# Attention into a two-layer MLP: tile 5's second layer by seven block products within tile 6's first layer, batches 4 to 7 prepared ahead, casts of v by ScalarE

## The chip, the cores and the metric

The kernel runs on one core of one Trainium2 chip. The metric is the device time of one execution in microseconds; the time of a kernel is the median of its runs. A profile is one more execution, taken by the hardware profiler; its times are in microseconds from the start of its span.

## The reference

Eight batches of eight heads, 576 positions of 64 channels, all inputs fp32. The softmax of q runs over the channels and that of k over the positions, so attention is two small products per head; the result, 4608 tokens of 512 features, goes through two dense layers with a leaky ReLU between them.

```python
q_s = np.exp(q - np.max(q, axis=-1, keepdims=True))
q_s = q_s / (np.sum(q_s, axis=-1, keepdims=True) + 1e-09)
k_s = np.exp(k - np.max(k, axis=2, keepdims=True))
k_s = k_s / (np.sum(k_s, axis=2, keepdims=True) + 1e-09)
kv = np.einsum('bhsd,bhse->bhde', k_s, v)
attn_out = np.einsum('bhsd,bhde->bhse', q_s, kv)
x = attn_out.transpose(0, 2, 1, 3).reshape(B * S, H * D)   # 4608 x 512
h = x @ w_in                                               # w_in 512 x 2048
g = np.maximum(0.01 * h, h)
out = g @ w_out                                            # w_out 2048 x 512
```

## The kernel before

**The dense layers.** The 4608 tokens are nine tiles of 512 (TT). x is kept transposed in SBUF as `xT`, bf16. Layer 1 of a tile is 16 block rows j of four matmuls each (128x512, bf16, L563); after each block row ScalarE applies the leaky ReLU into a tile of `g_pool` (L572). Layer 2 is four blocks of 128 tokens (tsub) with 16 matmuls of 128x512 each (L584, driven by `layer2_at`, L983); after the sixteenth, ScalarE copies the bank to `out_sb` (L578) and SyncE issues two stores of 128 KB (L581). Tile 0 has an order of its own, tiles 1 to 5 run layer 1 and then layer 2 this way, and tile 6 only its layer 1. Tiles 7 and 8 are computed as a pair with Strassen-like products of 2x2 blocks (products at L998, tail at L1252). Such a scheme takes seven block products where the plain one takes eight; its sums of blocks need an fp32r operand. Tile 6's second layer is computed by seven block products too, in 112 matmuls of 256 columns (`fill_steps`, L1156 to L1165): two of the products are plain, in bf16, and five use a sum of blocks of g (6r1 to 6r4, 6c22) with a sum of blocks of `w_out` (v1 to v4, and o22, a copy). They fill gaps of the first layer of the pair.

**The attention of a batch.** Its steps are functions that each issue instructions to one engine:

- `load_all` (SyncE): k, q and v of a batch into the six buffers of `raw_pool`.
- `k_begin`, `k_tree` (VectorE, L160): the maximum of k, first by a tree of elementwise maxima over four halvings.
- `k_allmax` (VectorE, L167 to L190): the maximum across partitions, by transposes within blocks; then `k_sub` (VectorE, L198) and `k_exp` (ScalarE, L206), which leaves `ke`.
- `q_max` (L245), `q_sub` (L304) on VectorE, `q_exp` on ScalarE (L312), `q_sum` (L321) and `q_norm` (L328) on VectorE, which leave `qe`; `q_turn` then transposes `qe` into `qX` by a DMA transpose on SyncE's queue (L551).
- `v_cast`: v to bf16 in two halves, on GpSimd (L218) for most batches.
- `attend_kv(b)` (TensorE): k·v of batch b+1 (L341), and between its parts q·kv of batch b (L479). Then `kd_make` on VectorE (L361, L362) divides k·v by its sums, and ScalarE casts the result of batch b to `xT` (`x_keep`, L500). One PSUM tile, `pokv`, holds part of both, and `x_keep` reads it after `kd_make` has.

Inside `attend_kv(b)`, `ke` of b+1 is asked for at once and `qX` of b after the first 24 matmuls.

**The order.** Everything around the dense layers is placed by hand. `at(t, u, ...)` (L595) hangs functions on a slot, and `run(t, u)` (L600) issues them there. Slots u = 0 to 15 of tile t lie after block row u of layer 1; slots 16 + 4·tsub + j//4 lie in layer 2 after each fourth matmul, so a tile has 32. The instructions of each engine run in the order of issue, and an engine that waits holds back all that stands behind it; the loads, the transposes and the stores of the output share SyncE's one queue. The slots of each batch are set on L699 to L784: for batches 4 and 5 a loop over t = 3, 4 with the helpers `k_front` (L740), `q_front`, `casts` and `q_back`, for 6 and 7 by single lines. For the last three batches `attend_kv` stands at slot 23 of tiles 3, 4 and 5, and batch 7's attention at (5, 29).

**What the end of the kernel prepares.** The weight sums (`out_weight_tiles` L807, `out_weight_sums` L812, `in_weight_sums`, the last on GpSimd), the token sums of the pair (`token_sums`, L844) and the sums of tile 6's g (`six_sums`, `six_first`) hang on slots of tiles 5 and 6. `home` (L863) takes an fp32r buffer for a sum, and `spent(n)` (L793) names parts of `xT` whose tokens are no longer read, which take blocks of g near the end.

Of the kernel before, what the change touches and what calls it, by code (L numbers as in the profile page):

```python
# [20 lines left out]
L = 64  # L21
# [5 lines left out]
def kernel(  # L27
# [31 lines left out]
    g_pool = ctx.enter_context(tc.tile_pool(name="gsb", bufs=10))  # L59
# [752 lines left out]
    def out_weight_sums(*names):  # L812
        w = lambda fh, os: w_out_sb[:, fh * NH : (fh + 1) * NH, os]
        for n in names:
            if n == "o22":
                nc.gpsimd.tensor_copy(out=late["o22"], in_=w(1, E2))
                continue
            x, y = dict(
                v1=lambda: (w(0, E2), w(0, E1)),
                v2=lambda: (w(1, E2), plain("v1")),  # L820
                v3=lambda: (w(1, E2), w(0, E2)),
                v4=lambda: (w(1, E1), plain("v2")),
            )[n]()
            subtract(nc.vector, n, x, y)
# [19 lines left out]
    def token_sums():  # L844
# [4 lines left out]
        for n in ("s1", "s2", "s3", "s4", "a22"):  # L849
            late[n] = pool.tile([P, 2, TT], F32R, name=n)  # L850
        nc.vector.tensor_tensor(out=late["s1"], in0=xT[:, CL, XB], in1=xT[:, CR, XB], op=ALU.add)
# [14 lines left out]
    def six_blocks(h):  # L866
        hs = slice(h * M2, (h + 1) * M2)
        return [(slice(2 * k, 2 * k + 2), lambda fh, k=k: late["g6"][4 * fh + k][:, :, hs]) for k in range(4)]

    def six_sums(n, k):  # L870
        (ms, h0), (_, h1) = six_blocks(0)[k], six_blocks(1)[k]
        part = lambda n: late[n][:, ms].bitcast(FP32)
        if n == "c22":
            nc.scalar.copy(out=late["6c22"][:, ms], in_=h1(1))
            return
        x, y, op = dict(
            r1=lambda: (h1(0), h1(1), ALU.add),
            r2=lambda: (part("6r1"), h0(0), ALU.subtract),
            r3=lambda: (h0(0), h1(0), ALU.subtract),
            r4=lambda: (h0(1), part("6r2"), ALU.subtract),  # L880
        )[n]()
        eng = nc.vector if n in ("r1", "r2") else nc.gpsimd
        eng.tensor_tensor(out=late["6r2" if n == "r4" else "6" + n][:, ms], in0=x, in1=y, op=op)

    def six_first(k):
        if k == 0:
            home("6r1", "alpha")
            home("6r2", "beta")
        six_sums("r1", k)
        six_sums("r2", k)  # L890

    for n in range(3):
        at(6, 10 + 2 * n, lambda n=n: six_first(n))
    at(6, 14, lambda: pair_first(0))

    def g_tiles():
        return [g_pool.tile([P, 2, TT], BF16, name="gj") for _ in range(NF // 2)]
# [114 lines left out]

    for t in range(1, TA):
        g_sb = []
        for j in range(NF):
            ph = psB_pool.tile([P, TT], FP32, name="ph", tag=BANK_TAG)
            layer1(j, ph, t * TT, TT)
            if j % 2 == 0:
                g_sb.append(g_pool.tile([P, 2, TT], BF16, name="gj"))
                if t == TA - 1:  # L1020
                    late["g6"] = g_sb
            leaky(g_sb[j // 2][:, j % 2], ph)
# [10 lines left out]
    def g7_rows(i):  # L1033
        if i == 0:
            g7_pairs.extend(g_pool.tile([P, 2, TT], BF16, name="gj") for _ in range(2))
        for fh in range(2):
            if i < 2:
                g7[fh * NH + i] = g7_pairs[fh][:, i]
            elif i < 6:
                g7[fh * NH + i] = spent(4 * (4 + fh) + i - 2)  # L1040
# [3 lines left out]
    def g7_blocks(h):  # L1044
# [3 lines left out]
            (slice(2, 4), lambda fh: xT[:, 0:2, ts(4 + fh)]),  # L1048
            (slice(4, 6), lambda fh: xT[:, 2:4, ts(4 + fh)]),
            (slice(6, 8), lambda fh: xT[:, 2 * fh : 2 * fh + 2, ts(6)]),  # L1050
        )

    def g7_wide(h):
        b = g7_blocks(h)
        ts = lambda t: slice(t * TT + h * M2, t * TT + (h + 1) * M2)
        return b[0], (slice(2, 6), lambda fh: xT[:, :, ts(4 + fh)]), b[3]
# [11 lines left out]
    def sums_ahead(n, names=("r1",)):  # L1068
        if n == 0 and "r1" in names:
            home("r1", "beta")  # L1070
            late["r3lo"] = late["ahead"].tile([P, NH // 2, M2], F32R, name="r3lo")
        if n == 2 and "r3" in names:
            home("r3", "alpha")
# [13 lines left out]
    def pair_layer1(i, fills):  # L1087
# [17 lines left out]
        else:  # L1105
            six_first(3)
# [21 lines left out]
        if i + 2 < NH:  # L1128
            in_weight_sums(i + 2)
        if i == 1:  # L1130
            home("6r3", "alpha")
        for n in {1: (0, 1), 2: (2, 3)}.get(i, ()):
            six_sums("r3", n)
        for n in {3: range(4)}.get(i, ()):
            six_sums("r4", n)
# [13 lines left out]
    early, late_in = {}, {}  # L1149

    def put(o, t, half, i, cols, issues=(nc.sync, nc.sync)):
        for n, issue in enumerate(issues):
            b, c = divmod(t * TT + half * M2 + i * P + n * L, S)
            issue.dma_start(out=out_r[b, c // L, :, cols], in_=o[n * L : (n + 1) * L, cols])

    def fill_steps():  # L1156
        t, g = TA - 1, lambda n: late["g6"][n // 2][:, n % 2]
        o1, o2 = ([osb_pool.tile([P, O], FP32, name="out_sb") for _ in range(2)] for _ in range(2))
        bank2 = lambda: psO_pool.tile([P, 2, H2], FP32, name="pout", tag="pout")
        pw, py = bank2(), bank2()  # L1160

        def steps(ps, a, w, first=True):
            for i in range(2):
                for m in range(NH):
                    nc.tensor.matmul(  # L1165
                        ps[:, i],
                        lhsT=a(m)[:, i * P : (i + 1) * P],
                        rhs=w(m),
                        start=(first and m == 0 and i == 0),
                        stop=(m == NH - 1 and i == 1),  # L1170
                        skip_group_check=True,
                    )
                    if (i, m) != (1, NH - 1):
                        yield

        rows = lambda n: (lambda m: late[n][:, m])
        w_first = lambda fh: (lambda m: w_out_sb[:, fh * NH + m, E1])
        yield from steps(pw, lambda m: g(NH + m)[:, 0:M2], w_first(1))
        for i in range(2):
            nc.scalar.copy(out=o1[i][:, E1], in_=pw[:, i])  # L1180
        yield
        yield from steps(py, rows("6r1"), rows("v1"))
        yield
        px = bank2()
        yield from steps(px, lambda m: g(m)[:, 0:M2], w_first(0))

        def six_c11():
            for i in range(2):
                add(o1[i][:, E1], px[:, i], o1[i][:, E1])

        early[3] = six_c11
        yield
        yield from steps(px, rows("6r2"), rows("v2"), False)
        for i in range(2):
            nc.scalar.copy(out=o1[i][:, E2], in_=px[:, i])
        yield
        yield from steps(px, rows("6r3"), rows("v3"), False)
        for i in range(2):
            nc.scalar.copy(out=o2[i][:, E2], in_=px[:, i])

        def six_c22():
            for i in range(2):
                add(o2[i][:, E2], py[:, i], o2[i][:, E2])

        def six_cast():
            home("6c22", "alpha")
            for n in range(4):
                six_sums("c22", n)

        early[5], late_in[5] = six_c22, six_cast  # L1210
        yield
        yield from steps(py, rows("6r2"), rows("o22"), False)

        def six_c12():
            for i in range(2):
                add(o1[i][:, E2], py[:, i], o1[i][:, E2])
                put(o1[i], t, 0, i, slice(0, O))

        late_in[7] = six_c12
        yield  # L1220
        yield from steps(px, rows("6c22"), rows("v4"), False)
        for i in range(2):
            nc.scalar.copy(out=o2[i][:, E1], in_=px[:, i])
            put(o2[i], t, 1, i, slice(0, O))
        yield

    fill = fill_steps()
# [33 lines left out]
    def row_sums(wide, name, n, pool, op, x, y, eng=nc.vector):  # L1261
        if n == "r3":
            home("r3", "alpha")
# [13 lines left out]
    gu = lambda: g_pool.tile([P, 2, H2], FP32, name="gu", tag="gj")  # L1277
# [139 lines left out]
```

## Time and profile before

| | |
|---|---|
| time, median of 3 runs | 277.43 us (277.17 to 277.5) |
| the profiled execution's own time | 277.72 us |
| its span | 275.8 us |
| tile 3: layer 1, layer 2 | 105.89 to 119.70, to 134.81 |
| tile 4: layer 1, layer 2 | 134.81 to 148.62, to 163.73 |
| tile 5: layer 1, layer 2 | 163.73 to 177.54, to 193.37 |
| tile 6: layer 1 begins | 193.37 |

The times of the tiles are where the pieces of the chain of waits begin, in the profiled execution. How to read the rows that follow in the prediction: a row of the chain gives a start, a length, the engine, the output's name, the line, and how many instructions it joins; a row of an engine's timeline gives start, length, engine, line, operation and the names with their shapes, and in brackets the idle time before it and what ended that. In a row that groups instructions the three numbers are the shortest, the median and the longest duration in ns. "DMA to landing" is the time from the issue of a transfer to its completion.

### The profile page before, as it was taken

The page shows a single profiled execution, that of the slowest core. Times are in us where ns is not written, and L with a number is a line of the kernel's source. Part 1 is how long each engine was busy: PE and PEld are TensorE (multiplying, and loading weights), DVE is VectorE, ACT ScalarE, POOL GpSimd, SP SyncE. Part 2 cuts the span into 40 slices and gives each one's busy share as a digit, 9 for nine tenths or more (in the row PEclk, how much of TensorE's full clock was granted, in tenths as well). Part 3 has the DMA queues.
Part 4 walks back from the last instruction along what each step waited for, and adds up shares of the span by engine and source line. Part 5 has one row for each costly group of instructions (what it writes and reads, how often), then busy time and mean ns, then how long its engine had stood idle before and what let it go on. Part 6 is the DMA issues. An engine that isn't in the chain of part 4 may idle for free.

```text
span 275.8 us, 5326 instructions
## 1 busy us (share of the span) xinstructions
PE 268.4 (97%) x2041; PEld 156.3 (57%) x2066; DVE 220.8 (80%) x314; ACT 175.8 (64%) x322; POOL 89.9 (33%) x102
## 2 busy tenths in 40 slices
PE   8899999999999999999999999999999999999994
PEld 3478644444444544445444544454446777889994
DVE  2995995899999939984979799966997756669961
ACT  3977573785389366846486656854766767984241
POOL 2866470149103001200600069400001999840000
PEclk9999999999999999999999999999999999999999
DMA  6999999987998599069707956027100000025244
GB/s 236 337 209 320 242 273 244 390 275 242 235 382 292 50 347 346 16 133 391 231 0 141 384 190 126 0 49 153 39 0 0 2 0 2 1 52 117 62 107 124
DMA packets 40568, 46.48 MB, mean 168 GB/s; under 512 B 18912, under 2 KB 24288, under 8 KB 40544
## 3 DMA queue, kind: packets, MB, share of 16 engines
q1 hardware_dynamic: 36720, 41.56, 50.5%
q0 software_dynamic: 3504, 4.20, 8.7%
q10 hardware_dynamic: 320, 0.39, 0.4%
q8 instruction: 16, 0.26, 0.4%
q14 instruction: 8, 0.07, 0.1%
HBM read 36.70 MB, written 9.44 MB: 167 GB/s over the span
## 4 chain that ended last, share of the span: by engine, by line
PE 93%; DVE 3%; DMA 2%; issue 1%; ACT 0%; SPq 0%
PE ph L563 35%; PE pout L584 30%; PE pq L1252 9%; PE pp L998 9%; PE pout L1165 5%; DMA k_raw<-in_k_dram 2%; PE po L479 2%; DVE t L160 1%; PE pokv L341 1%; PE pkv L341 1%; PE pkv L419 0%; DVE k_raw L410 0%; ACT ke L206 0%; DVE kmax L160 0%; DVE kd L434 0%
## 5 line engine op out<-in xcount | busy, mean ns | idle before, releaser
L563 PE MATMUL ph<-xT,w_in_sb 128*128 128x512 bf16 (+1 forms) x504 | 98.4, 352 | 0.4
L584 PE MATMUL pout<-w_out_sb,gj 128*128 128x512 bf16 x371 | 84.6, 379 | 0.9 <-issue 0.3
L563 PEld LDWEIGHTS <-w_in_sb 128*128 128x128 bf16 x512 | 49.8, 98 | 47.0 <-DMA w_in_sb<-in_moe_w_in_dram 0.3
L572 ACT ACTIVATE gj<-ph 128x512 bf16<-128x512 f32 x112 | 63.6, 601 | 19.2 <-PE ph L563 18.6
L584 PEld LDWEIGHTS <-gj 128*128 128x128 bf16 x384 | 36.7, 98 | 43.6 <-issue 0.2
L218 POOL CAST vb<-v_raw 128x1152 bf16<-128x1152 f32 x13 | 19.2, 1505 | 81.7 <-DMA v_raw<-in_v_dram 64.5
L578 ACT COPY out_sb<-pout 128x512 f32<-128x512 f32 x20 | 11.7, 584 | 30.3 <-PE pout L584 19.1
L206 ACT ACTIVATE ke<-k_raw 128x2304 bf16<-128x2304 f32 (+2 forms) x13 | 18.0, 1385 | 7.2 <-DVE k_raw L198 6.7
L328 DVE TENSOR_TENSOR qe<-qe,qrec 128x2304 bf16<-128x2304 bf16 (+5 forms) x13 | 21.8, 1680 | 0.4
L321 DVE TENSOR_REDUCE qsum<-qe 128x36 f32<-128x2304 bf16 (+5 forms) x13 | 20.0, 1541 | 2.4 <-ACT qe L312 2.2
L245 DVE TENSOR_REDUCE qmax<-q_raw 128x36 f32<-128x2304 f32 (+5 forms) x13 | 20.0, 1539 | 0.8 <-DMA q_raw<-in_q_dram 0.8
L312 ACT ACTIVATE qe<-q_raw 128x2304 bf16<-128x2304 f32 (+5 forms) x13 | 17.2, 1321 | 4.3 <-POOL q_raw L304 3.4
L198 DVE TENSOR_TENSOR k_raw<-k_raw,kall 128x1152 f32<-128x1152 f32 (+2 forms) x10 | 18.7, 1885 | 0.3
L304 POOL TENSOR_TENSOR q_raw<-q_raw,qmax 128x512 f32<-128x512 f32 (+3 forms) x7 | 11.8, 1682 | 21.2 <-DVE qmax L245 19.3
L799 POOL TENSOR_TENSOR t<-w_in_sb 128x256 fp32r<-128x256 bf16 x16 | 15.5, 971 | 0.0
L500 ACT CAST xT<-po 128x448 bf16<-128x448 f32 (+3 forms) x31 | 13.3, 513 | 2.5 <-PE po L479 2.5
L1095 DVE COPY u<-pp 128x512 f32<-128x512 f32 x8 | 5.5, 691 | 10.9 <-PE pp L998 10.9
L998 PE MATMUL pp<-s,t 128*128 128x512 f32 x48 | 13.9, 398 | 0.0
L160 DVE TENSOR_TENSOR t<-t 128x256 f32<-128x256 f32 (+2 forms) x22 | 13.3, 605 | 0.7
L304 DVE TENSOR_TENSOR q_raw<-q_raw,qmax 128x2304 f32<-128x2304 f32 (+1 forms) x6 | 13.2, 2202 | 0.2
L1124 POOL COPY gate<-u 128x1 f32<-128x1 f32 x1 | 0.2, 189 | 37.5 <-DVE u L1001 37.5
L160 DVE TENSOR_TENSOR t<-k_raw 128x512 f32<-128x512 f32 (+1 forms) x11 | 11.2, 1015 | 1.3 <-DMA k_raw<-in_k_dram 1.2
(155 smaller groups left out, 381.3 us busy)
## 6 DMA issues: line engine op xcount, KB each, us to landing
out_dram<-out_sb SPq DMA_DIRECT2D x60, 128.0 KB, 3.9
k_raw<-in_k_dram SPq DMA_DIRECT2D x8, 576.0 KB, 6.0
v_raw<-in_v_dram SPq DMA_DIRECT2D x8, 576.0 KB, 8.9
q_raw<-in_q_dram SPq DMA_DIRECT2D x4, 1152.0 KB, 9.1
v_raw<-in_v_dram SPq DMA_DIRECT2D x4, 1152.0 KB, 11.8
k_raw<-in_k_dram SPq DMA_DIRECT2D x4, 1152.0 KB, 6.7
q_raw<-in_q_dram SPq DMA_DIRECT2D x4, 576.0 KB, 7.7
w_in_sb<-in_moe_w_in_dram POOLq DMA_DIRECT2D x7, 256.0 KB, 6.8
```

The costliest lines, as they stand in the source:

```text
L160: nc.vector.tensor_tensor(out=o, in0=i0, in1=i1, op=ALU.max)
L198: eng.tensor_tensor(out=ks, in0=ks, in1=st[b]["kall"][:, hs].unsqueeze(2).to_broadcast([P, n, R, D]), op=ALU.subtract,)
L218: eng.tensor_copy(out=o, in_=i)
L245: nc.vector.tensor_reduce(out=o, in_=st[b]["q"][:, hs, rs], axis=AX.X, op=ALU.max)
L304: eng.tensor_tensor(out=qs, in0=qs, in1=st[b]["qmax", rs.start, hs.start].unsqueeze(3).to_broadcast([P, m, n, D]), op=ALU.subtract,)
L321: nc.vector.reduce_sum(out=qsum, in_=q_cols(b, rs, hs), axis=AX.X)
L328: nc.vector.tensor_tensor(out=qes if out is None else out, in0=qes, in1=st[b]["qrec", rs.start, hs.start].unsqueeze(3).to_broadcast([P, n, ...
L563: nc.tensor.matmul(ph, lhsT=w_in_sb[:, cb, j * P : (j + 1) * P], rhs=xT[:, cb, c0 : c0 + n], start=(cb == 0 and first), stop=(cb == NB - 1 ...
L572: nc.scalar.activation(out=o, in_=ph, func=AF.Prelu, alpha=LEAKY_SLOPE)
L584: nc.tensor.matmul(pout, lhsT=g_sb[j // 2][:, j % 2, tsub * P : (tsub + 1) * P], rhs=w_out_sb[:, j, os], start=(j == 0), stop=(j == NF - 1),)
L998: nc.tensor.matmul(ps, lhsT=w(c), rhs=a(c), start=(first and c == 0), stop=(c == 1), skip_group_check=True)
L1252: nc.tensor.matmul(ps[i], lhsT=a(m)[:, i * P : (i + 1) * P], rhs=w(m), start=(first and m == 0 and (each or i == 0)), stop=(m == NH - 1 an ...
```

## The change

Tile 5's second layer is no longer 64 matmuls of 128x512 in four blocks. It is the seven products that tile 6 has, now by one function for both (`seven_steps`): 112 matmuls of 256 columns, 32 plain in bf16 and 80 with fp32r sums. Eight of them follow tile 5's layer 1, then batch 7's attention, then 24 more; the other 80 come in groups of 16 behind block rows 5, 7, 9, 12 and 14 of tile 6's layer 1. The sums of tile 5's g (5r1 to 5r4) are made by VectorE and 5c22 by ScalarE. Tile 5's g is kept in the parts of `xT` that tiles 0 to 3 have left (`spent`), the second half of tile 6's g in those of tiles 4 and 5; `g_pool` becomes three pools of 4, 4 and 2 buffers, which also take some of the sums. Some of tile 6's sums move from VectorE to GpSimd.

The slots of batches 4 to 7 move. `attend_kv(4)`, `(5)` and `(6)` go from slot 23 of tiles 3, 4 and 5 to (3, 18), (4, 17) and (4, 28); the maximum of k is taken one to several slots earlier, and `k_max(7)` at (4, 9) stands ahead of `q_ready(6)`. Load 6 goes to (3, 8) and load 7 to (3, 31), both in the order k, v, q; `q_turn(4)` and `q_turn(5)` stand directly ahead of them, `q_turn(6)` at (4, 20) behind tile 4's first store, `q_turn(7)` at (5, 9). The casts of v of batches 5, 6 and 7 and the copy o22 go from GpSimd to ScalarE.

```diff
-    g_pool = ctx.enter_context(tc.tile_pool(name="gsb", bufs=10))
+    g_pools = [ctx.enter_context(tc.tile_pool(name=f"gsb{n}", bufs=b)) for n, b in enumerate((4, 4, 2))]
...
-    for t in range(3, B - 3):
-        b = t + 1
-        q_front(b, t - 1, 29)
-        at(t, 2, lambda b=b: q_exp(b, ALLR))
-        k_front(b + 1, t, 1, 8)
-        casts(b + 1, t, 6)
-        at(t, 17, lambda b=b: k_exp(b + 1, ALLH))
-        at(t, 23, lambda b=b: attend_kv(b))
-        q_back(b, t, 5)
-        at(t, 5, lambda b=b: load_all(b + 2))
-    q_front(6, 4, 18)
-    at(4, 26, lambda: q_exp(6, ALLR))
-    k_front(7, 4, 29, 40)
-    q_back(6, 5, 1)
-    q_front(7, 5, 2)
-    casts(7, 5, 6)
-    at(5, 12, lambda: q_exp(7, ALLR))
-    q_back(7, 5, 16)
-    at(5, 17, lambda: k_exp(7, ALLH))
-    at(5, 23, lambda: attend_kv(6))
+    def k_max(b, t, u):
+        at(t, u, lambda: k_begin(b), lambda: q_begin(b), lambda: k_tree(b, ALLH))
+
+    def k_less(b, t, u):
+        at(t, u, lambda: k_allmax(b), lambda: k_sub(nc.vector, b, ALLH))
+
+    def q_ready(b, t, u):
+        at(t, u, lambda: q_sum(b, ALLR), lambda: q_norm(b, ALLR))
+
+    def casts_act(b, *slots):
+        for gg, (t, u) in enumerate(slots):
+            at(t, u, lambda gg=gg: v_cast(nc.scalar, b, gg))
+
+    q_front(4, 2, 20)
+    k_max(5, 2, 28)
+    at(2, 30, lambda: q_exp(4, ALLR))
+    q_ready(4, 2, 30)
+    casts_act(5, (3, 4), (3, 8))
+    at(3, 8, lambda: q_turn(4), lambda: load_all(6, "kvq"))
+    k_less(5, 3, 8)
+    at(3, 14, lambda: k_exp(5, ALLH))
+    q_front(5, 3, 14)
+    at(3, 18, lambda: attend_kv(4))
+    k_max(6, 3, 19)
+    at(3, 20, lambda: q_exp(5, ALLR))
+    q_ready(5, 3, 20)
+    casts_act(6, (3, 28), (3, 30))
+    at(3, 31, lambda: q_turn(5), lambda: load_all(7, "kvq"))
+    k_less(6, 3, 31)
+    at(4, 4, lambda: k_exp(6, ALLH))
+    q_front(6, 4, 4)
+    at(4, 9, lambda: q_exp(6, ALLR))
+    k_max(7, 4, 9)
+    q_ready(6, 4, 9)
+    at(4, 17, lambda: attend_kv(5))
+    k_less(7, 4, 18)
+    at(4, 20, lambda: q_turn(6))
+    casts_act(7, (4, 20), (4, 22))
+    at(4, 24, lambda: k_exp(7, ALLH))
+    q_front(7, 4, 24)
+    at(4, 28, lambda: attend_kv(6))
+    at(5, 0, lambda: q_exp(7, ALLR))
+    at(5, 0, lambda: out_weight_tiles(), lambda: out_weight_sums("v1"))
+    q_ready(7, 5, 0)
+    at(5, 9, lambda: q_turn(7))
...
-                nc.gpsimd.tensor_copy(out=late["o22"], in_=w(1, E2))
+                nc.scalar.copy(out=late["o22"], in_=w(1, E2))
...
-    at(5, 26, out_weight_tiles, lambda: in_weight_sums(0), lambda: in_weight_sums(1))
-    at(5, 26, lambda: out_weight_sums("o22", "v1"))
+    at(5, 10, lambda: out_weight_sums("v2", "v3"))
+    at(5, 12, lambda: in_weight_sums(0), lambda: in_weight_sums(1))
+    at(6, 3, lambda: out_weight_sums("o22"))
...
-    at(5, 29, lambda: attend_all(B - 1, (R7, both), (RE, both)), token_sums)
-    at(6, 4, lambda: out_weight_sums("v2", "v3", "v4"))
...
+    at(6, 0, lambda: five_sums("5r3"), lambda: out_weight_sums("v4"))
+    at(6, 5, lambda: five_steps(16))
+    at(6, 6, lambda: five_sums("5r4", "alpha"), token_sums)
+    at(6, 7, lambda: five_steps(16))
+    at(6, 8, lambda: five_sums("5c22", "beta"))
+    at(6, 9, lambda: five_steps(16))
+    at(6, 10, lambda: spare("6r1"), lambda: seven_sums("6r1", 0))
+    at(6, 12, lambda: five_steps(16), lambda: seven_sums("6r1", 1), lambda: six_second(0))
+    at(6, 14, lambda: five_steps(16), lambda: seven_sums("6r1", 2), lambda: six_second(1))
     at(6, 14, lambda: pair_first(0))
...
+        pw = bank2()
+        yield from steps(pw, lambda m: g(NH + m)[:, 0:M2], w_first(1))
+        keep_all(o1, E1, pw)
+        yield
+        if late_first:
+            px = bank2()
+            yield from steps(px, lambda m: g(m)[:, 0:M2], w_first(0))
+            add_all(o1, E1, px)
+            yield
+        py = bank2()
+        yield from steps(py, rows("r1"), v("v1"))
...
+        yield from steps(px, rows("r2"), v("v2"), False)
+        keep_all(o1, E2, px)
+        yield
+        yield from steps(px, rows("r3"), v("v3"), False)
...
+        yield from steps(py, rows("r4"), v("o22"), False)
...
+        yield from steps(px, rows("c22"), v("v4"), False)
...
     for t in range(1, TA):
...
             layer1(j, ph, t * TT, TT)
...
+            if t == TA - 2:
+                leaky(spent(j), ph)
+            elif t == TA - 1 and j >= NH:
+                leaky(spent(16 + j - NH), ph)
...
             run(t, j)
-        for tsub in range(NTS if t < TA - 1 else 0):
+        for tsub in range(NTS if t < TA - 2 else 0):
             for _ in layer2_at(t, g_sb, tsub):
                 pass
+        if t == TA - 2:
+            five = seven_steps(t, spent, late_first=True)
+            five_steps = lambda n: [next(five) for _ in range(n)]
+            five_steps(8)
+            attend_all(B - 1, (R7, both), (RE, both))
+            late_pools()
+            five_sums("5r1", "alpha")
+            five_sums("5r2", "beta")
+            five_steps(24)
...
+        if i == 0:
+            six_second(2, nc.gpsimd)
+            six_second(3, nc.gpsimd)
         if i == 1:
...
+            home("6r3", "beta")
+            for n in range(4):
+                seven_sums("6r3", n, nc.gpsimd)
+        if i == 3:
+            late["6r4"] = late["6r2"]
+            for n in range(4):
+                seven_sums("6r4", n, nc.gpsimd)
```

More of the change, by code (lines that the diff above doesn't have):

```diff
@@ L863, in home, with spare @@
     def home(n, buf):
         late[n] = late["ahead"].tile([P, NH, M2], F32R, name=n, tag=buf)
-    def six_blocks(h):
-        hs = slice(h * M2, (h + 1) * M2)
[L868 to L874, printed above, removed]
+    def spare(n):
+        late[n] = [g_pools[1].tile([P, 2, M2], F32R, name=n, tag="gj") for _ in range(NH // 2)]
@@ L1034, in g7_rows @@
         if i == 0:
-            g7_pairs.extend(g_pool.tile([P, 2, TT], BF16, name="gj") for _ in range(2))
+            g7_pairs.extend(gj(8) for _ in range(2))
+        if i == 2:
+            late["g7"] = [gj(4) for _ in range(4)]
         for fh in range(2):
@@ L1039, in g7_rows @@
             elif i < 6:
-                g7[fh * NH + i] = spent(4 * (4 + fh) + i - 2)
+                g7[fh * NH + i] = late["g7"][2 * fh + (i - 2) // 2][:, i % 2]
             else:
@@ L1105, in pair_layer1 @@
         else:
-            six_first(3)
+            seven_sums("6r1", 3)
         between(fills[0])
@@ L1147, in pair_third @@
         add(u2, py, u2)
[L1149 to L1225, printed above, removed]
@@ L1227 @@
-    fill = fill_steps()
+    fill = seven_steps(TA - 1, g6)
     def between(n):
@@ L1262, in row_sums @@
         if n == "r3":
-            home("r3", "alpha")
+            home("r3", "beta")
         else:
```

167 lines of the change are left out of this document (129 added, 38 removed).

## The prediction

> **What bounds the kernel now.** I read the page's busy shares first, then the chain that ended last, then that chain over tiles 3 to 7 in order of time.
>
> ```profile
> span 275.8 us, 5326 instructions
> PE 268.4 (97%) x2041; PEld 156.3 (57%) x2066; DVE 220.8 (80%) x314; ACT 175.8 (64%) x322; POOL 89.9 (33%) x102
> PEclk9999999999999999999999999999999999999999
> PE 93%; DVE 3%; DMA 2%; issue 1%; ACT 0%; SPq 0%
> 119.70 4.53 PE pout L584 x21
> ...
> 134.81 4.10 PE ph L563 x19
> ...
> 148.62 1.08 PE pout L584 x5
> ...
> 155.53 0.31 PE pokv L341 x24
> ...
> 157.04 0.05 issue
> ...
> 163.73 4.10 PE ph L563 x19
> ...
> 177.54 1.08 PE pout L584 x5
> ...
> 190.92 0.61 PE po L479 x16
> ...
> 193.37 0.65 PE ph L563 x3
> ```
>
> TensorE is the bound: 97% busy at the full granted clock, and 93% of the chain. In the stretch that the change touches, the chain holds nothing but PE work and pieces of "issue" of 0.05 us; no transfer and no other engine is late there. So time is won only by shorter PE work, and lost as soon as one operand arrives after PE asks for it. Three lengths come from these rows. Layer 1 of tile 4 is 64 matmuls in 148.62 - 134.81 = 13.81 us, 0.216 each. Its layer 2 takes 163.73 - 148.62 = 15.11, of which 64 x 0.216 = 13.82 are matmuls; the other 1.29 is one attend_kv. Tile 5's second layer, 177.54 to 193.37, is again 13.82 plus an attend_kv and batch 7's attention.
>
> **PE work: the gain.** Tile 5's 64 second-layer matmuls become 112 of 256 columns, 32 in bf16 and 80 with an fp32r weight and token operand (r1·v1, r2·v2, r3·v3, r4·o22, c22·v4). Tile 6 already runs both kinds:
>
> ```profile
> 219.95 1.76 PE pout L1165 x16
> ...
> 224.90 1.92 PE pout L1165 x16
> ...
> 230.03 1.92 PE pout L1165 x16
> ```
>
> The first row is a bf16 group, 1.76/16 = 0.110 each; the others are fp32r, 1.92/16 = 0.120. New cost 32 x 0.110 + 80 x 0.120 = 13.12; removed 13.82: **-0.7 us**. Nothing else is taken from PE: both attend_kv and the attention of batch 7 only move.
>
> By the Trainium skill, "TensorE: Matmul & The Clock Gate", section "Back-to-back issue gap", a matmul's gap depends on its columns alone, N/2.4 + 2.5 ns, 109 ns at 256; the fp32r rows above disagree by 11 ns each, and the measurement decides. By that rule the 112 would take 12.2 and the gain would be 1.6 us, an estimate from the page, and the forecast below would come out 0.9 lower.
>
> **What hides the new side work.** ACT takes six casts of v (each half of k_exp's elements, so about 1.1 us by its 2.12 below) and the o22 copy; it is 64% busy and the casts stand in second layers, where it has few rows to evict. DVE takes 5r1 to 5r4, 8 x 1024 elements at 1.22 (the row at 84.30), and four adds of 256, about 12 us in all, within the 13.1 us of the products and the 13.8 of tile 6's layer 1 between which they lie. PE reaches the product of r4 behind 80 of the 112 and 13 of tile 6's block rows, some 21 us after tile 5's layer 1; by the same 1.22 steps, with the sums of w_out and of tokens that stand between, r4 is done about 1 us before. I cost them at nothing. If VectorE's sums were stretched as the tree at 108.27 was beside POOL's casts (below, 4.42 in place of 2.78), 5r4 would be about 1 us late; but those casts leave POOL, which speaks against it, and POOL has little else to do there.
>
> **Preparing ahead: where a wait comes in.** Batches 4 to 7 move up by up to a tile, and each keeps a queue in front of it. I laid SP, DVE and ACT out in the new order from tile 3 on, with these durations:
>
> ```profile
> 84.30 1.22 DVE L160 TENSOR_TENSOR t<-k_raw 128x1024 f32<-128x1024 f32 x1
> ...
> 87.08 2.54 DVE L321 TENSOR_REDUCE qsum<-qe 128x36 f32<-128x2304 bf16 x1
> ...
> 90.08 2.56 DVE L328 TENSOR_TENSOR qe<-qe,qrec 128x2304 bf16<-128x2304 bf16 x1
> 92.55 0.44 DVE L167 STREAM_TRANSPOSE kmaxT<-kmax 128x256 f32<-128x256 f32 x1
> ...
> 102.40 0.17 DVE L361 RECIPROCAL krec<-pokv 128x2 f32<-128x2 f32 x1 [4.06 <-PE pokv L479]
> ...
> 103.21 2.54 DVE L245 TENSOR_REDUCE qmax<-q_raw 128x36 f32<-128x2304 f32 x1
> ...
> 108.27 1.22 DVE L160 TENSOR_TENSOR t<-k_raw 128x1024 f32<-128x1024 f32 x1
> ...
> 112.69 2.54 DVE L321 TENSOR_REDUCE qsum<-qe 128x36 f32<-128x2304 bf16 x1
> ...
> 118.16 0.43 DVE L167 STREAM_TRANSPOSE kmaxT<-kmax 128x256 f32<-128x256 f32 x1
> ...
> 120.46 2.56 DVE L198 TENSOR_TENSOR k_raw<-k_raw,kall 128x2304 f32<-128x2304 f32 x1
> ```
>
> Starts give steps: tree 2.78 (84.30 to 87.08), q_sum with its reciprocal 3.00, q_norm 2.47, kd 0.81 (102.40 to 103.21), lanes of k 2.30 (118.16 to 120.46), k_sub 2.56.
>
> The first late thing is **k of batch 7**. Load 7 is issued on SP at (3,31), the last hook of tile 3, behind tile 3's last stores and behind q_turn(5):
>
> ```profile
> 125.67 10.94 SPq L581 DMA_DIRECT2D out_dram<-out_sb  x8
> 145.78 2.71 SPq L551 DMA_TRANSPOSE qX<-qe  x1
> 148.53 1.10 SPq L84 DMA_DIRECT2D k_raw<-in_k_dram  x2
> ```
> ```profile
> L84 SPq DMA_DIRECT2D k_raw<-in_k_dram x2: 467/524/582, 148.5 to 149.2; - x2
> ...
> DMA to landing us min/median/max: 4.8/5.3/5.7
> ```
>
> The stores end at 136.61. In the trace a transpose at 145.78 has the second half of k behind it on the ground at 149.2 + 5.7 = 154.9, 9.1 later; so k7 is there at 136.6 + 9.1 = 145.7. In the hand-written order its tree stands on DVE at (4,9) ahead of q_sum(6). DVE is free for it at about 143.3 (attend_kv(4) starts behind 12 second-layer matmuls, 119.70 + 2.6 = 122.3, and its kd(4) ends 1.29 + 0.81 later at 124.4; then tree(6), q_sum(5), q_norm(5), lanes, k_sub, q_max, q_sub by the steps above, some 19 us), so it waits about 2.4 us. Behind it queue q_sum(6), q_norm(6), kd(5), k_sub(7), and behind kd(5) on ACT the copies out of the shared PSUM tile and tile 4's first output, and behind that on SP q_turn(6).
>
> 145.7 + tree 2.78 + q_sum 3.00 + q_norm 2.47 = 154.0; kd(5) ends 154.8; lanes 157.1; k_sub(7) 159.7; k_exp(7) on ACT:
>
> ```profile
> 123.05 2.12 ACT L206 ACTIVATE ke<-k_raw 128x2304 bf16<-128x2304 f32 x1 [2.71 <-DVE k_raw L198]
> ...
> 157.79 0.70 ACT L500 CAST xT<-pokv 128x256 bf16<-128x256 f32 x2
> ...
> 160.36 0.63 ACT L578 COPY out_sb<-pout 128x512 f32<-128x512 f32 x1
> ```
>
> ends at 161.85. PE reaches attend_kv(6), which now stands behind the 52nd matmul of tile 4's layer 2 with attend_kv(5) ahead of it, at 148.62 + 52 x 0.216 + 1.29 = 161.14. **Stall 0.7 us.**
>
> The second is **q_turn(6)**, same place. kd(5) 154.8, copy out of the shared tile 0.35, output copy 0.6, two store issues 1.1 (as the two of k above): the transpose is issued at 156.9. How long it takes to land the trace shows from 4.6 to 6.2:
>
> ```profile
> L551 SPq DMA_TRANSPOSE qX<-qe x1: 2709/2709/2709, 145.8 to 145.8; - x1
> ...
> DMA to landing us min/median/max: 4.6/4.6/4.6
> ```
> ```profile
> L551 SPq DMA_TRANSPOSE qX<-qe x1: 2712/2712/2712, 167.2 to 167.2; - x1
> ...
> DMA to landing us min/median/max: 6.2/6.2/6.2
> ```
> ```profile
> qX<-qe SPq DMA_TRANSPOSE x7, 5.8
> ```
>
> The 4.6 had loads issued right behind it, the 6.2 had none, and q_turn(6) and q_turn(7) have none either; I take the median 5.8 and keep both ends. qX6 is there at 161.5, 162.7 or 163.1. PE wants it 0.3 after the start of attend_kv(6) (24 matmuls, the 0.31 row): 161.44. So at that place the stall is 0.7 (k_exp alone decides), **1.3** or 1.7.
>
> By the Trainium skill, "DMA: Bandwidth & Descriptors", section "Latency and other measured facts", a DMA transpose moves 261 GB/s on top of some 2 us fixed; 128 x 2304 bf16 is 0.59 MB, so 2.3 + 2 = 4.3 us, an estimate. The 4.6 row agrees and the 6.2 row does not; the page's figure belongs to the second rival below.
>
> The third is **q_turn(7)**, at (5,9). From tile 5's layer 1 start S: first block row and leaky about 1.5, q_exp(7) 2.13 (the size of k_exp), q_sum 3.00, q_norm 2.5: issued at S + 9.15, there at S + 13.75, 14.95 or 15.35. PE wants it after 64 + 8 matmuls (the 8 are 0.87), S + 14.7: stall 0, **0.3** or 0.7.
>
> **Sum** at 5.8: -0.7 + 1.3 + 0.3 = +0.9 us. The profiled run's own time is 277.72 (span 275.8 and 1.9 around it), 0.29 above the median 277.43 of the three runs shown; from the median the forecast is **278.3 us**.
>
> **The rivals.** *All covers hold* (faster): k7 lands 1.3 us earlier than by the row, or 0.7 with transposes of 4.6, and only the -0.7 is left: 276.7. For it speaks that the first two stalls hang on one landing, which I read from one load to about 1 us; against it, that the row it is read from has no stores moving ahead of it, as load 7 has. *k alone*: the transposes land in 4.6, and only ke7 stalls, 0.7: -0.7 + 0.7, so 277.4, no change. For it speaks the row at 145.8; against it that this one had loads behind it. *Both transposes late*: 6.2 each, 1.7 + 0.7 - 0.7 = +1.7: 279.1. For it speaks the row at 167.2, which like these had no load behind it, and that q_turn(6) has two stores of 128 KB just ahead on its queue; against it, that half of the seven landed in 5.8 or less. It decides from a landing of about 6 up. That the engine which becomes the bound is DVE, in tile 6's layer 1, with r4 late by the 1 us above, gives 277.4 - 0.7 + 1 = 277.7 and lies within the others' range; I give it no chance of its own.
>
> **How the numbers follow.** Forecast (5.8) 0.33; both late 0.20; k alone 0.20; all hidden 0.27. What a measurement here can tell from no change is 0.2%, 0.55 us: below 276.9 is faster, above 278.0 slower. So faster 0.27, same 0.20, slower 0.33 + 0.20 = 0.53. The range takes in the ends of the unknown landings: 276.6 to 279.3; the likeliest case's own is 277.8 to 278.8, half a microsecond for the landings to each side.
>
> **What would show it.** Right: a PE idle ahead of an L341 or L479 matmul at about 161, released by ACT's ke and then by the transpose; a DVE idle of about 2 us ahead of a tree at 143 to 146 released by the load of k; the 112 matmuls at 0.110 and 0.120. Wrong: a chain with no such gap and a span shorter by 0.7 (all hidden); a gap ahead of an fp32r product in tile 6's layer 1 (DVE's sums late); a stall already in tile 3, where by the same steps k_exp(5) ends some 0.7 us before attend_kv(4) needs it and I cost it at nothing.

## The result and the profile after

| | before | changed |
|---|---|---|
| median | 277.5 us (277.04 to 278.04, 20 executions) | 278.09 us (277.69 to 280.32, 20 executions) |
| profiled execution | 277.72 us, span 275.8 | 277.69 us, span 275.7 |

The ratio is 1.0028, 95% interval 1.0016 to 1.0041: the changed kernel is slower by about 0.6 us. Two things stand in this table beside the median. The spread of the changed kernel is 2.6 us where before's is 1.0, and its profiled execution is its fastest: what follows is read from an execution 0.4 us under the median.

From the page of the changed kernel, first part and fourth (the chain that ended last):

```profile
span 275.7 us, 5464 instructions
PE 269.0 (98%) x2114; PEld 162.9 (59%) x2114; DVE 225.9 (82%) x330; ACT 184.9 (67%) x336; POOL 81.8 (30%) x97
...
PE 85%; DVE 8%; DMA 4%; ACT 1%; SPq 1%; issue 0%; DVEq 0%
```

The chain was 93% PE; now it is 85%, and DVE and DMA have 8% and 4%. That is what a chain looks like that leaves TensorE once: where PE waited, it turns off to what was late and follows it back as far as it was late. The chain in order of time shows where (start, length, engine, what):

```profile
134.43 4.33 PE ph L563 x20
...
139.80 5.44 DMA k_raw<-in_k_dram
...
145.33 1.24 DVE t L160
...
156.74 2.57 DVE k_raw L198
159.34 2.13 ACT ke L206
...
161.51 0.38 PE pokv L341 x24
...
165.48 13.81 PE ph L563 x64
...
179.29 0.97 PE pout L1094 x8
...
180.88 2.73 PE pout L1094 x24
...
188.79 1.90 PE pout L1094 x16
...
206.16 0.45 PE pp L1062 x2
```

PE is left at 138.76 and met again at 161.51, at `attend_kv(6)`. Between lie the load of k of batch 7, its tree, q_sum(6), q_norm(6), kd(5), and then k_allmax, k_sub and k_exp of batch 7. What PE waited for, from 40 us to the end, is one line (waited for: total us, times, longest):

```profile
PE pokv L341 <- ACT ke L206: 0.8, 1, 0.8
```

VectorE's timeline and SyncE's queue carry the same chain; the bracket is the idle time ahead of the instruction and what ended it:

```profile
140.20 2.56 DVE L304 TENSOR_TENSOR q_raw<-q_raw,qmax 128x2304 f32<-128x2304 f32 x1
145.33 1.23 DVE L160 TENSOR_TENSOR t<-k_raw 128x1024 f32<-128x1024 f32 x1 [2.56 <-DMA k_raw<-in_k_dram]
```
```profile
136.34 2.78 SPq L551 DMA_TRANSPOSE qX<-qe  x1
139.16 1.11 SPq L84 DMA_DIRECT2D k_raw<-in_k_dram  x2
...
155.45 1.12 SPq L581 DMA_DIRECT2D out_dram<-out_sb  x2
156.68 2.89 SPq L551 DMA_TRANSPOSE qX<-qe  x1
```

The prediction had this to within half a microsecond, forecast first: transpose at 136.6 (136.34), k7 on the ground at 145.7 (139.80 + 5.44 = 145.2), 2.4 us of idle VectorE (2.56), ke7 at 161.85 (161.47), a gap of 0.7 (0.8), q_turn(6) at 156.9 (156.68). What it did not have is the transposes, q_turn(6) and then q_turn(7):

```profile
L551 SPq DMA_TRANSPOSE qX<-qe x1: 2891/2891/2891, 156.7 to 156.7; - x1
...
DMA to landing us min/median/max: 4.7/4.7/4.7
```
```profile
L551 SPq DMA_TRANSPOSE qX<-qe x1: 2687/2687/2687, 174.9 to 174.9; - x1
...
DMA to landing us min/median/max: 4.5/4.5/4.5
```

4.7 and 4.5 us in place of 5.8: neither stops PE. In this execution the rival "k alone" is what happened, and its time, 277.69, is near that rival's 277.4.

### The profile page after: what moved, and what is told of

Read it like the earlier page. It is cut to its first block, busy times and chain, and to the rows that moved or that the text cites. A ratio compares the mean times of both kernels' runs of the same rounds, so it can differ in the third digit from the quotient of the medians.

```text
span 275.7 us, 5464 instructions
## 1 busy us (share of the span) xinstructions
PE 269.0 (98%) x2114; PEld 162.9 (59%) x2114; DVE 225.9 (82%) x330; ACT 184.9 (67%) x336; POOL 81.8 (30%) x97
## 4 chain that ended last, share of the span: by engine, by line
PE 85%; DVE 8%; DMA 4%; ACT 1%; SPq 1%; issue 0%; DVEq 0%
PE ph L563 32%; PE pout L584 21%; PE pout L1094 10%; PE pq L1343 10%; PE pp L1062 9%; DMA k_raw<-in_k_dram 4%; DVE t L160 2%; PE po L479 1%; ACT ke L206 1%; DVE k_raw L198 1%; DVE qe L328 1%; DVE qsum L321 1%; PE pkv L341 1%; PE pokv L341 1%; PE pkv L419 0%; DVE k_raw L410 0%
## 5 line engine op out<-in xcount | busy, mean ns | idle before, releaser
L563 PE MATMUL ph<-xT,w_in_sb 128*128 128x512 bf16 (+1 forms) x512 | 99.5, 353 | 0.0
L584 PE MATMUL pout<-w_out_sb,gj 128*128 128x512 bf16 x320 | 71.4, 379 | 0.0
L572 ACT ACTIVATE gj<-ph 128x512 bf16<-128x512 f32 x88 | 49.1, 605 | 13.7 <-PE ph L563 13.1
L584 PEld LDWEIGHTS <-gj 128*128 128x128 bf16 x320 | 30.6, 98 | 36.1 <-issue 0.2
L824 POOL TENSOR_TENSOR t<-w_in_sb 128x256 fp32r<-128x256 bf16 x16 | 12.3, 772 | 68.7 <-DMA out_dram<-out_sb 68.7
L578 ACT COPY out_sb<-pout 128x512 f32<-128x512 f32 x16 | 9.4, 589 | 16.5 <-PE pout L584 13.4
L572 ACT ACTIVATE xT<-ph 128x512 bf16<-128x512 f32 x24 | 13.9, 605 | 5.9 <-PE ph L563 5.8
L500 ACT CAST xT<-po 128x448 bf16<-128x448 f32 (+3 forms) x31 | 13.2, 509 | 4.4 <-PE po L479 4.4
L824 POOL TENSOR_TENSOR t<-w_in_sb,t 128x256 fp32r<-128x256 bf16 x16 | 15.1, 943 | 0.6
L218 POOL CAST vb<-v_raw 128x1152 bf16<-128x1152 f32 x7 | 9.8, 1436 | 17.1 <-DMA v_raw<-in_v_dram 17.1
L160 DVE TENSOR_TENSOR t<-k_raw 128x512 f32<-128x512 f32 (+1 forms) x11 | 10.2, 930 | 3.7 <-DMA k_raw<-in_k_dram 3.6
```

The costliest lines, as they stand in the source:

```text
L563: nc.tensor.matmul(ph, lhsT=w_in_sb[:, cb, j * P : (j + 1) * P], rhs=xT[:, cb, c0 : c0 + n], start=(cb == 0 and first), stop=(cb == NB - 1 ...
L572: nc.scalar.activation(out=o, in_=ph, func=AF.Prelu, alpha=LEAKY_SLOPE)
L584: nc.tensor.matmul(pout, lhsT=g_sb[j // 2][:, j % 2, tsub * P : (tsub + 1) * P], rhs=w_out_sb[:, j, os], start=(j == 0), stop=(j == NF - 1),)
L824: eng.tensor_tensor(out=late[o], in0=a, in1=b, op=ALU.subtract)
```

## The experiments

The theory after the first reading: the seven products gain what the PE rows say, and the wait for k of batch 7 gives it back and makes the time vary. The rivals: late transposes in the slower executions, side work of the products that eats their gain, VectorE's order, ScalarE's casts.

**Load k of batch 7 early** (`e1_k7_early`)

```diff
-    at(3, 31, lambda: q_turn(5), lambda: load_all(7, "kvq"))
+    at(3, 24, lambda: load_all(7, "k"))
+    at(3, 31, lambda: q_turn(5), lambda: load_all(7, "vq"))
```

> Load of k for batch 7 issued at (3, 24), ahead of q_turn(5) and of the last stores of tile 3; nothing else changes. If the wait for k7 is what costs the changed kernel its gain, k7 lands by about 134, the tree of batch 7 starts right behind q_sub(6) near 142.7 in place of 145.3, ke of batch 7 is there by about 159.5, PE has no gap at attend_kv(6), and the time falls by the 0.8 us of that gap: about 277.2, ratio to before 0.998 or a little under. If the excess sits elsewhere (transposes that land late, VectorE's sums in tile 6, the clock), the gap goes but the time stays near 278.1, ratio 1.002 to 1.003.

276.88 us (276.73 to 277.09), before 277.33, ratio 0.9985, interval 0.9976 to 0.9994. VectorE's timeline and the chain:

```profile
140.30 2.56 DVE L304 TENSOR_TENSOR q_raw<-q_raw,qmax 128x2304 f32<-128x2304 f32 x1
142.77 1.22 DVE L160 TENSOR_TENSOR t<-k_raw 128x1024 f32<-128x1024 f32 x1
```
```profile
134.51 10.58 PE ph L563 x49
...
164.72 8.20 PE ph L563 x38
...
205.41 0.45 PE pp L1063 x2
```

The tree has no bracket any more. From tile 4's layer 1 to tile 5's takes 164.72 - 134.51 = 30.21 us, against 165.48 - 134.43 = 31.05 in the changed kernel: 0.84 us, the gap. The spread is 0.4 us over eleven executions; the changed kernel had 1.6 over eleven in the same session (below).

**Only the order on SyncE's queue** (`e5_k_before_turn`)

```diff
-    at(3, 31, lambda: q_turn(5), lambda: load_all(7, "kvq"))
+    at(3, 31, lambda: load_all(7, "k"), lambda: q_turn(5), lambda: load_all(7, "vq"))
```

> At (3, 31) the two issues of k for batch 7 go ahead of q_turn(5); the rest of load 7 stays behind it. If k7 is late because of the transpose ahead of it on SyncE's queue, it lands some 3 us sooner, near 142, the tree starts behind q_sub(6) with no idle time, PE has no gap at attend_kv(6), and the time equals that of the early load: 276.9, ratio 0.9985, with a spread under 0.5 us. If the stores of tile 3 are what delays it, k7 still lands after 144 and half of the gap or more stays: 277.4 or more.

276.87 us (276.69 to 277.36), before 277.32, ratio 0.9985, interval 0.9976 to 0.9993. The load of k, and the tree on VectorE:

```profile
L84 SPq DMA_DIRECT2D k_raw<-in_k_dram x2: 500/544/587, 136.2 to 136.8; - x2
...
DMA to landing us min/median/max: 4.5/5.1/5.7
```
```profile
142.62 1.22 DVE L160 TENSOR_TENSOR t<-k_raw 128x1024 f32<-128x1024 f32 x1
```

k is issued at 136.2 and 136.8 and its second half needs 5.7 us, so it lands at 142.5 where the changed kernel had 145.2, the tree starts with no idle time, and PE waits for no other engine. The transpose ahead of the load was the delay that counts. The stores delay the load too: ahead of them, in `e1_k7_early`, it landed at 135.7. But VectorE is free for the tree only near 142.7, and the time is no shorter there. Two issues that change places turn the change from slower into faster than before. The spread, 0.67 us, missed the 0.5 of the expectation.

**The products undone, k late and k early** (`e2_plain_five`, `e4_plain_k7`). Both compute tile 5's second layer as before, in 64 matmuls; the second loads k as `e1_k7_early` does.

```diff
...
-            five = seven_steps(t, spent, late_first=True)
+            pairs5 = [xT[:, 2 * m % NB : 2 * m % NB + 2, m // 2 * TT : (m // 2 + 1) * TT] for m in range(NF // 2)]
+            five = (u for tsub in range(NTS) for u in layer2_at(t, pairs5, tsub))
...
-            five_steps(8)
+            five_steps(4)
             attend_all(B - 1, (R7, both), (RE, both))
             late_pools()
-            five_sums("5r1", "alpha")
-            five_sums("5r2", "beta")
-            five_steps(24)
+            five_steps(60)
```

> Tile 5's second layer as before (64 matmuls of 512 columns in one go, no sums of its g), all the rest of the change kept. If the seven products gain what the PE rows say, this loses 0.6 to 0.7 us against the changed kernel: about 278.75, ratio 1.0045 to 1.005. If their side work eats the gain, it is equal to the changed kernel or faster: 278.1 or less, ratio 1.002 or less.

> Both edits: k of batch 7 loaded at (3, 24) and tile 5's second layer as before. With the wait theory and the gain from the products independent of each other, this stands to the early-k kernel as the plain-layer kernel stands to the changed one, 0.6 to 0.7 us slower, and close to before: 277.4 to 277.9, ratio 1.000 to 1.001. If the earlier preparation costs something beyond the wait for k7, it stays slower than before by more: ratio 1.002 or above.

With k early: 277.64 us (277.56 to 277.77), before 277.33, ratio 1.0011, interval 1.0002 to 1.002; 0.76 slower than with the products. Its chain:

```profile
134.31 10.58 PE ph L563 x49
...
164.53 8.20 PE ph L563 x38
...
205.83 0.43 PE pp L1059 x2
```

From tile 5's layer 1 to the first product of the pair: 205.83 - 164.53 = 41.30 us here, 205.41 - 164.72 = 40.69 with the products. So they gain 0.61 us by the rows, and 0.62 in the changed kernel (206.16 - 165.48 = 40.68). Before's own row of the first product of the pair is this:

```profile
206.32 0.43 PE pp L998 x2
```

From the prediction's row at 163.73 to 206.32 is 42.59 with an attend_kv of 1.29 in it, again 41.30. With k early and the layer as before, the kernel is still 0.3 us slower than before; no row shown here accounts for that, and the cause stays open.

With k late: 279.88 us (279.38 to 280.36), ratio 1.0092, interval 1.0078 to 1.0106. That is 2.2 us over the changed kernel of the same session, far from the 0.6 to 0.7 expected, and taken as a price of the products it would be wrong by a factor of three. Its chain, and ScalarE's timeline at the end:

```profile
139.61 6.35 DMA k_raw<-in_k_dram
...
166.21 8.20 PE ph L563 x38
...
207.51 0.43 PE pp L1058 x2
```
```profile
271.28 1.93 ACTq L1081 DMA_DIRECT2D out_dram<-gu  x1
```

207.51 - 166.21 = 41.30: the products are worth the 0.62 here too. The rest lies elsewhere. k of batch 7 took 6.35 us from its second issue in place of 5.44, and PE waited 1.6 us in place of 0.8:

```profile
PE pokv L341 <- ACT ke L206: 1.6, 1, 1.6
```

And at the end ScalarE took 1.93 us to issue one store: from TensorE's last matmul to the end of the span it is 5.0 us, in the changed kernel 3.7. The last two experiments are about that. Together 0.62 + 0.8 + 1.3 = 2.7, the distance between the two profiled executions (280.36 and 277.69).

**The changed kernel once more** (`after_again`)

> The changed kernel once more, for its spread: its twenty executions lay between 277.7 and 280.3, before's between 277.0 and 278.0. If transposes that land late make the difference between its fastest and its median, a second profile near the median shows a transpose of 5.5 us or more and a gap at attend_kv(6) of over 0.8 us; if it is the clock, the granted clock is under 1.0 where the time is high. Median 278.1, ratio 1.002 to 1.003.

277.71 us (277.47 to 279.09), ratio 1.0021, interval 1.0011 to 1.0032. In its profile q_turn(6) and q_turn(7) landed in 4.7 and 4.6 us, and PE waited for ke again:

```profile
PE pokv L341 <- ACT ke L206: 0.6, 1, 0.6
```

The median, 0.4 us under the first session's 278.09, missed the expected 278.1, and the kernel loses 0.4 us to before here in place of 0.6. This profiled execution, 277.86 us, lies near the median and shows no late transpose, so the expectation of late transposes falls as far as one profile can tell. The clock does not carry it either: among the first twenty executions the slowest had 0.985 (280.32 us) and 0.993 (279.56), but 278.85, 278.73 and 278.6 us were reached at 1.000.

**VectorE's order** (`e6_tree_behind`)

```diff
-    k_max(7, 4, 9)
     q_ready(6, 4, 9)
+    k_max(7, 4, 9)
```

> At (4, 9) the tree of batch 7 goes behind q_sum(6) and q_norm(6) on VectorE. If the place of the waiting tree in VectorE's order were what costs (other work held back behind it), the idle 2.6 us would be filled and the gap go: 276.9. By the layout it is not: q_exp(6) ends on ScalarE at 145.9 in the changed kernel, so q_sum(6) cannot start before 146.0, the chain to ke of batch 7 ends some 0.6 us later than now, the gap grows to about 1.4 us and the time to 278.4 or so, ratio 1.003 to 1.005.

278.4 us (278.12 to 278.56), before 277.32, ratio 1.0039, interval 1.0026 to 1.0052. The waits of PE:

```profile
PE pokv L341 <- ACT ke L206: 1.4, 1, 1.4
```

The 1.4 us of the expectation. The idle time ahead of the tree could not be filled with the work behind it, because q_exp(6) ends only at 145.9 in the changed kernel; here VectorE stood idle for 3.2 us, until 145.7, for that. So the tree's place in the order was not the fault; that its operand's arrival was is shown by the two experiments with an earlier load.

**Ask later** (`e7_attend_later`)

```diff
-    at(4, 28, lambda: attend_kv(6))
+    at(4, 30, lambda: attend_kv(6))
```

> attend_kv(6) from (4, 28) to (4, 30), 8 matmuls or 1.73 us later; nothing else changes. If PE only asks too soon for ke of batch 7, the gap of 0.6 to 0.8 us goes in the profile: 276.9 to 277.1, ratio 0.9985 to 0.999, though the load's late landings still show in single executions above that. If the later attend_kv(6) holds up what stands behind it (the copies to xT, kd(6), q_exp(7) and so q_turn(7)), the gap comes back ahead of batch 7's attention and the time stays at 277.7 or above.

277.3 us (276.77 to 277.97), before 277.32, ratio 0.9999, interval 0.999 to 1.0008; its profiled execution is the slowest, 277.97. The waits of PE there, and the row of q_turn(7):

```profile
PE po L479 <- DMA qX<-qe: 0.9, 1, 0.9
...
PE pout L584 <- ACT out_sb L578: 0.2, 1, 0.2
```
```profile
L551 SPq DMA_TRANSPOSE qX<-qe x1: 2692/2692/2692, 175.9 to 175.9; - x1
...
DMA to landing us min/median/max: 4.5/4.5/4.5
```

The wait for ke is gone and one of 0.9 us stands ahead of batch 7's attention: q_turn(7) is issued at 175.9, 10.9 us after tile 5's layer 1 begins in place of 9.4. k of batch 7 landed late as well, 6.6 us after its second issue. This expectation was half met: the median gained 0.4 us on the changed kernel, and the rival's gap appeared.

**Casts of v on GpSimd** (`e3_casts_pool`)

```diff
-            at(t, u, lambda gg=gg: v_cast(nc.scalar, b, gg))
+            at(t, u, lambda gg=gg: v_cast(nc.gpsimd, b, gg))
```

> The six casts of v of batches 5, 6 and 7 back on GpSimd, in the same slots; o22 stays on ScalarE. If the casts are hidden on either engine, nothing moves: ratio 1.002 to 1.003 as the changed kernel. If GpSimd's casts stretch VectorE's elementwise work beside them (k_sub of batch 7 from 2.56 to about 3.1, and the sums of q), the gap at attend_kv(6) grows by 0.5 to 1 us: 278.4 or more, ratio 1.004 or above.

281.37 us (280.85 to 281.65), before 277.32, ratio 1.0143, interval 1.013 to 1.0157. The waits of PE, and ScalarE's timeline at the end:

```profile
PE pokv L341 <- ACT ke L206: 1.5, 1, 1.5
PE pout L584 <- ACT out_sb L578: 1.3, 1, 1.3
```
```profile
271.79 2.32 ACTq L1085 DMA_DIRECT2D out_dram<-gu  x1
```

Dearer than either theory said. In this one profile, two costs sit on the chain behind k. The casts of batch 7, held back on GpSimd until 147.2, run beside the tree, whose last two steps take 1.26 and 1.25 us there and 0.44 and 0.43 in the changed kernel; kd(5) ends at 156.5 in place of 154.5. The copies behind it on ScalarE then free tile 4's output bank too late, and PE waits a second time. The third cost is at the end, as in `e2_plain_five`: 5.2 us from TensorE's last matmul to the end of the span, in place of 3.7.

**The two causes apart** (`e8_pool_k_first`, `e9_pool_k_fill`). The first has the casts on GpSimd and k ahead of q_turn(5), by the edits shown above; the second adds eight copies of one column on ScalarE.

```diff
     at(5, 9, lambda: q_turn(7))
+    at(6, 2, lambda: [nc.scalar.copy(out=warm, in_=ident[:, 0:1]) for _ in range(8)])
```

> The casts of v on GpSimd together with k of batch 7 issued ahead of q_turn(5). In the kernel with the casts on GpSimd alone PE lost 1.5 and 1.3 us around attend_kv(6), and at the end ScalarE's issue of a store took 2.32 us in place of 0.56, beside a fetch of its instructions at 272.5. If the two losses on PE came through the wait for k7, they go here, and what is left over the kernel with k first (276.87) is the end, some 1.5 us: 278.2 to 278.5, ratio 1.003 to 1.004. If the casts on GpSimd cost by themselves (VectorE's operations stretched beside them), a gap at attend_kv(6) stays and the time is 279 or more.

> The same with eight copies of one element per partition on ScalarE at (6, 2), whose results nobody reads: they shift ScalarE's later instructions by eight places. If the fetch of instructions in the midst of the last stores is what costs 1.5 us at the end, it now falls some eight instructions sooner, near 266 to 268, the last issues take 0.5 us each again and the time is 276.9 to 277.1, ratio 0.9985 to 0.999. If the fetch only stands beside a cost of another origin, the end stays as long as in the kernel without the copies.

Without the copies 278.67 us (278.11 to 278.77), before 277.23, ratio 1.0045, interval 1.0031 to 1.0058. With them 276.96 us (276.74 to 277.24), before 277.23 too, ratio 0.9989, interval 0.998 to 0.9998. In neither did PE wait. ScalarE's timeline at the end, without and with:

```profile
268.98 2.40 ACTq L1085 DMA_DIRECT2D out_dram<-gu  x1
```
```profile
268.75 0.56 ACTq L1086 DMA_DIRECT2D out_dram<-gu  x1
```

And the DMA traffic from 268.5 to 273.5 without them, by queue:

```profile
q10 hardware_dynamic: 80, 0.13, 12.1%
q14 instruction: 1, 0.01, 0.6%
```

One fetch on queue 14 falls among the last stores; with the copies it has come some 7 us sooner and that window holds none. So where k is in time, the casts cost nothing that shows on either engine (276.96 us here; 276.87 with the casts on ScalarE, in another session, each just under its own before). And 1.7 us hang on the eight copies: the last fetch of ScalarE's instructions no longer falls among the stores. The mean granted clock, 0.995 without the copies and 1.000 with them, is no rival: from 30 to 270 us it is 1.00 in both, so it can't slow TensorE's work there, and TensorE ends at the same time in both (271.2 and 271.1 us).

## Why the prediction was right

The range, the direction and the size held: 278.3 forecast, 278.09 measured. Point by point, the gain and the stall for k were right, the two transposes were wrong, and that the sum came out so near is in part luck.

- **The gain of the products.** Forecast 0.7 us, measured 0.62 from the trace and 0.76 between two kernels with k early. By the trace it is a little under, because the groups of the 112 take 13.2 us in the chain (0.97 + 2.73 + 1.90 + 4 x 1.91), not 13.1: the 32 plain ones took 0.116 us each in place of 0.110, the 80 with fp32r 0.119. By an estimate from the Trainium skill's rule ("TensorE: Matmul & The Clock Gate", "Back-to-back issue gap") the gain would have been 1.6; the fp32r groups took 1.90 to 1.91 us again, and the rows decide.
- **The stall for k of batch 7.** Forecast 0.7, measured 0.8 and 0.6 in the two profiles of the changed kernel, by the same chain: SyncE's order, the landing, 2.6 us of idle VectorE, q_sum, q_norm, kd, k_sub, k_exp. It is undone by two edits that both put the load ahead of q_turn(5), one also ahead of the stores; the first stands 0.83 us under the changed kernel of its session (276.88 to 277.71). One sum on the way was loose: the steps that the prediction lists between kd(4) and the tree add up to 18.2 us, not "some 19", so VectorE would be free at 142.6 and idle for 3.1 us. It was free at 142.8, and idle for 2.6 because k landed half a microsecond sooner than forecast.
- **q_turn(6) and q_turn(7).** Here the step "I take the median 5.8 and keep both ends" failed: the landings were 4.7 and 4.5, so the 0.6 us more at `attend_kv(6)` and the 0.3 us at batch 7's attention were not there. The ground given for it, that a transpose with no loads behind it is slow, is refuted by these two, which had none; and before's own trace has the opposite case, a transpose at 92.78 with loads right behind it that landed in 5.8. What goes with the late landings is in the traces: a fetch of instructions beside the transpose. Before's late one and the changed kernel's q_turn(7), by queue over the time of each:

```profile
q1 hardware_dynamic: 2336, 0.59, 50.3%
q8 instruction: 1, 0.02, 0.9%
```
```profile
q1 hardware_dynamic: 2336, 0.59, 70.1%
```

  The packets of both take the same time, 3.2 us (50.3% of a window of 6.3 us, 70.1% of one of 4.5), so it is the landing that comes late. In the twelve profiles, transposes later than 80 us, five in each, with a fetch on queue 8 or 14 while they were under way landed in 5.3 to 6.2 us (25 of them), those without in 4.5 to 4.7 (32); three more, with a load of k directly ahead, took 7.1 to 7.2. All the fetches began 2.3 to 4.2 us after the issue, before a quick transpose would have landed, so they are not found beside the late ones merely because those last longer. But the 25 are not independent: 23 of them are the same two transposes, near 92 and 112 us, in one kernel after the other. That the fetch is the cause, and not a mark of something else, was not tried for the transposes. The estimate of 4.3 us that the prediction works out from the Trainium skill ("DMA: Bandwidth & Descriptors", "Latency and other measured facts") is nearest to the second kind, 0.2 to 0.4 us under it.
- **The sum.** -0.7 + 1.3 + 0.3 was forecast; the profiled execution shows -0.62 + 0.8. Its time is 0.03 us under before's all the same, because tile 4 already begins 0.38 sooner (134.43 against 134.81), which neither term covers. The 0.9 us that separates the forecast from the rival "k alone" was all transposes, and they cost nothing in either profile of the changed kernel: that the first session's median, 278.09, came near 278.3 is luck as far as they go, and the second session's 277.71 lies nearer to the rival's 277.4. What may bring the first median to the forecast is a term that I had as one number: the landing of k of batch 7. In the six profiles with the load behind the transpose, it came 5.25 to 6.6 us after the second issue. Why it varies was not tried. With the load on the path, a later landing goes into the time (5.25, 5.44 and 6.35 us came with waits of PE of 0.6, 0.8 and 1.6); with it early, the spread is 0.4 us in place of 1.6 in the same session. The single executions between 278 and 280 us have no trace, so that all of their excess is this landing is argued, not shown; for the two slowest the lower clock is another candidate.
- **The covers at nothing.** The sums of VectorE for the products cost nothing: PE waited for none of them. The casts on ScalarE cost nothing, and beside a late k they cost about 2 us on GpSimd (281.37 - 277.71, less the 1.6 of the end; PE waited 2.8 us there in place of 0.8).

## What to carry to other kernels

When work is moved ahead, follow the load that feeds it through the queue on which it is issued: a DMA transpose ahead of it delayed this one by 2.7 us, and changing the two about made a change that lost 0.6 us in one session and 0.4 in another gain 0.45. Look at the spread beside the median: here it was 2.6 and 1.6 us with the load on the critical path, 0.4 and 0.7 with the load early, and 0.4 in `e6_tree_behind`, where another wait has taken its place. And an edit that is undone to find its price can shift something else: read the stage in the trace before the difference of two medians is taken as its price.

## What the runs showed of the hardware

- **A fetch of ScalarE's instructions among the last stores costs 1.3 to 1.7 us.** Three kernels ended this way (`e2_plain_five`, `e3_casts_pool`, `e8_pool_k_first`): one store issue took 1.93, 2.32 and 2.40 us where 0.56 is usual, and from TensorE's last matmul to the end of the span it was 5.0, 5.2 and 5.4 us in place of 3.7. In the changed kernel and in all the experiments a fetch of 8 KB on queue 14 begins behind the 447th to 450th row that the trace has of ScalarE: with 11 rows still to come in these three kernels, 15 in those that ended as usual, 19 with the eight copies. A shorter program brings it nearer to the end, but its length is not all: `e4_plain_k7` has the same work on ScalarE as `e2_plain_five`, but 15 rows behind its fetch and the usual end; why was not looked for. Eight copies of one column, 0.19 us each on an engine with time to spare, moved the fetch and brought the time from 278.67 to 276.96. The Trainium skill ("Runtime: NRT & Kernel Launch", "Instruction fetch mechanics") calls the crossing of a block mostly hidden; at this place it was not.
- **Transposes of the same 0.59 MB land in two groups**, 4.5 to 4.7 us and 5.3 to 6.2, the later ones with a fetch of instructions beside them, as told above; that the fetch is the cause is not shown.
- **GpSimd's casts beside VectorE's elementwise maxima** went with a stretch of the last steps of the tree, of 256 elements, from 0.43 to 1.25 us (the profile of `e3_casts_pool`).
